# A spectrum's return from DRAM cut into growing blocks, output blocks in halves, and the order around them rewritten

## The chip, the cores and the metric

One core of a Trainium2 chip runs one program. Its five engines work side by side, each through its own list of instructions in order: PE (TensorE, matrix products), ACT (ScalarE), DVE (VectorE), POOL (GpSimd) and SP (SyncE, which issues the transfers). The metric is the time of one execution in microseconds on the device, the median of the runs.

## The reference, cut to what matters

Input q is normalised and modulated, gates a long convolution, and the sum goes through a second normalisation and a gated linear unit. S = 2048 rows, D = 448 channels, F = 1792; all float32.

```python
mod = (_silu(c) @ w_mod).reshape(c.shape[0], 6, 1, -1)
sa, ca, ga, sb, cb, gb = ...
h = _layernorm(x) * (1 + ca) + sa            # LN1, modulation
k_shift = short causal convolution of k (4 taps); kv = k_shift * v
y = irfft(rfft(kv) * rfft(ssm_k))[:S] + kv * ssm_D
x = x + ga * (h * y)
h = _layernorm(x) * (1 + cb) + sb            # LN2, modulation
x = x + gb * ((sigmoid(h @ w_gate) * (h @ w_up)) @ w_down)
```

## The kernel before, in words

The channels are worked in two halves of 224 (h = 0 and 1), the 2048 rows as 16 tiles of 128 rows. The FFT is made of small matrix products. Stage 1 transforms along one axis; `av[h]`, 128 partitions x 32 slots x 224 channels, holds the spectrum of kv, `ak[h]` that of the filter. Between stages the 32 x 32 blocks of (row in a group of 32 partitions, slot) must be transposed. For some channel blocks DVE does that (`turn`, line 181, and the transposing read at line 339); for the first 112 channels of each half a return trip through DRAM does it: slots are written out to `kd0` or `kd1` and read back with row and slot exchanged.

The stretch that matters is `stage2_v` (line 306): 16 late steps p = 8h + n, eight channel blocks for each half. In each step PE makes the block's products `s2v` (line 316), DVE multiplies them with the filter's spectrum (`m`, line 320), PE transforms the product of the step before (`sa`, line 336, in `stage2_back`), which ACT copies into `av` (line 341) or DVE transposes into it (line 339). Then `beside` (line 682) does what else stands in that step, by tables on p: `TURNS`, the sums of the modulation vectors (`mod_parts`, `mod_sum`), the filter's own `s2k` products and ACT's copy of them (`stage2_k`, line 287; copy at line 291), LN1's statistics on ACT (`ln1_stats`, line 449; two tiles at a time, each a sum and a sum of squares), LN1's reciprocal and product on DVE (`ln1_end`, line 459), the gates on POOL and ACT (`gates`, line 466), and from step 12 on one output block of the first half per step (`stage_out`, line 354: 16 products; one call makes y0 for four tiles, written `y0_0` to `y0_3`; y1 is the second half's).

The second half's trip goes so: `eight_out` (line 346) writes eight slots of all 128 partitions to `kd1` in each of the steps 9 to 12, and in step 13 `half_in` (line 349) reads back all 32 slots in four transfers, one for each group of 32 partitions, 1024 pieces of 448 bytes each. These are issued by SP, in order, on one queue. The program uses eight DMA semaphores in turn: an issue waits until the transfer eight issues before it has landed, and everything behind it on SP waits too.

After step 15 come the last transform sa7, the y1 blocks (the first needs the returned spectrum), the vectors of modulation 3 and 5, the second half's gate, LN2's statistics (`ln2_stats`), the normalised rows (`norm_rows`), the turns of four row tiles through PE (`turn_one`, line 951; column group 1 is 64 wide and is turned twice, once for each half of the partitions, with a transpose and a product), and then the products of gate and up (`gu`, line 1004) with weights that are split into a high and a low part (`plain_hi` on ACT, `plain_lo`, line 532, on POOL for three of the first four pieces). From there on PE goes from gate products to down products (`d`, line 925) to the end.

Everything runs in the written order (`tc.manual_schedule()`, line 536): no scheduler moves anything. Buffers in PSUM are named by tags; tag `y`, `sa` and two of `t` go round.

Of the kernel before, what the change touches and what calls it, by code (L numbers as in the profile page):

```python
# [17 lines left out]
P = 128  # L18
C = 224
# [60 lines left out]
def adaln_conv_glu_kernel(ctx: ExitStack, tc: tile.TileContext, q, kT, v, ssm, shift, dskip,  # L80
# [225 lines left out]
    def stage2_v(between, last):  # L306

        for h in range(2):
            for n in range(8):
# [14 lines left out]
                between(h, n)  # L324
        last()
        stage2_back()

    def stage2_back():
# [3 lines left out]
        for b in range(2):  # L332
            for ex in range(2):
                r = slice(64 * ex, 64 * ex + 64)
                y = pt[r, b, :D] if not straight else pt[r, b].rearrange("p (j c) -> p j c", c=32)[:, :, :28]
                PE.matmul(y, wa[:, b, r], m[b][:, ex], start=True, stop=True)  # L336
# [4 lines left out]
        ACT.activation(block(av[h], h, n), cols4(rows(pt), h, n), AF.Copy)  # L341
# [4 lines left out]
    def eight_out(a, scratch, n, c):  # L346
        nc.sync.dma_start(scratch[:, 8 * n:8 * n + 8, c], a[:, 8 * n:8 * n + 8, c])

    def half_in(a, scratch, c, *bs):
        x = scratch.rearrange("(b q) p c -> b p q c", b=4)  # L350
        for b in bs:
            nc.sync.dma_start(a[32 * b:32 * b + 32, :, c], x[b, :, :, c])

    def stage_out(h, i, tag, cs=slice(0, C), pt=None):

        pt = two(tag, f"y{h}_{i}") if pt is None else pt
        for b in range(2):
            for jj in range(2):
                g = 4 * i + 2 * b + jj
                for s in range(2):  # L360
                    PE.matmul(pt[64 * s:64 * s + 64, b, jj * C + cs.start:jj * C + cs.stop], wb[:, 16 * s + g], av[h][:, 16 * s + g, cs], start=True, stop=True)  # L361
        return rows(pt)
# [33 lines left out]

    def mod_parts(m, tag, part=None):

        pr = two(tag, f"mod{m}")
        for h in range(2):  # L400
# [3 lines left out]
        if part is None:  # L404
            part = late["rb"].tile([P, D], F32, tag="part", bufs=1, name=f"part{m}")
        ACT.activation(part, pr[:, 0, :D], AF.Copy)
        mods[m] = pr, part

    def mod_sum(m):

        pr, part = mods.pop(m)
        if m not in (3, 4):
            PE.matmul(pr[:, 1, :D], ones, part, start=True, stop=True)
            if m == 2:
                DVE.tensor_mul(arow, arow, pr[:, 1, :D])
                DVE.tensor_mul(brow, brow, pr[:, 1, :D])
            else:
                ACT.activation({1: arow, 0: brow, 5: gbrow}[m], pr[:, 1, :D], AF.Copy, bias=1.0 if m == 1 else 0.0)
            return
        at, add = (0, 1.0) if m == 4 else (5, 0.0)  # L420
# [27 lines left out]

    def ln1_stats(k):

        for i in range(2 * k, 2 * k + 2):
            t, g = late["x1"][:, i], slice(i, i + 1)
            ACT.activation(gbrow, t, AF.Copy, scale=-1.0 / D, accum_out=nmr[:, g])
            ACT.activation(gbrow, t, AF.Square, bias=nmr[:, g], accum_out=rstd[:, g])
        if k % 2:
            r = rstd[:, 2 * k - 2:2 * k + 2]
            ACT.activation(r, r, AF.Sqrt, bias=eps, scale=1.0 / D)

    def ln1_end(i):
        r, m = rstd[:, 4 * i:4 * i + 4], nmr[:, 4 * i:4 * i + 4]  # L460
        DVE.reciprocal(r, r)
        DVE.tensor_mul(m, m, r)

# [210 lines left out]
    for n in range(2):  # L674
# [4 lines left out]
    TURNS = {0: ((0, 2),), 1: ((0, 3), (1, 0)), 2: ((0, 4), (1, 1)), 3: ((0, 5),), 4: ((0, 6), (1, 2)), 5: ((0, 7),), 6: ((1, 3),),  # L679
             9: ((0, 4), (1, 4)), 10: ((0, 5), (1, 5)), 11: ((1, 6),), 12: ((1, 7),)}  # L680

    def beside(h, n):

        p = 8 * h + n
        if p in (3, 4, 7, 10):
            ln1_end({3: 0, 4: 1, 7: 2, 10: 3}[p])
        for at in TURNS.get(p, ()):
            turn(av[at[0]], at[1])
        for m in {0: (0,), 1: (1,), 3: (2,), 10: (4,)}.get(p, ()):
# [28 lines left out]
        if p in (0, 1, 2, 3, 5, 6, 8, 9):  # L718
            ln1_stats(p if p < 4 else p - 1 if p < 7 else p - 2)
        if p >= 12:  # L720
            y = stage_out(0, p - 12, "y")
            if p < 14:
                gate(0, p - 12, y_copy(0, p - 12, y), POOL)
            elif p == 14:
                y = late["g02"] = y_copy(0, 2, y)
                POOL.tensor_mul(y, y, pairs(gt[0, 2]))
            else:
                late["y03"] = y

    def first_forms():  # L730
        late["g03"] = copy_home(3)
        DVE.tensor_mul(late["g03"], pairs(gt[0, 3]), late["y03"])
# [8 lines left out]
    plain_hi(0, 3)  # L741
    parts = slice(0, 7 * 28), slice(7 * 28, C)
    y10 = [stage_out(1, 0, "t", parts[0])]
    mod_parts(3, "sa")
    mod_parts(5, "y", gbrow)
    y10.append(stage_out(1, 0, "t", parts[1]))
    four = lambda x, c: pairs(x).rearrange("p b (j c) -> p b j c", c=C)[:, :, :, c]
# [3 lines left out]
    for c in parts:  # L751
        xs_ = late["x1"][:, 0:4, C + c.start:C + c.stop]
        DVE.tensor_add(xs_, xs_, gt[1, 0][:, :, c])
    mod_sum(3)
    mod_sum(5)
    gate_wd(0)
    yc = []
    y1 = [None, stage_out(1, 1, "t")]
    y1.append(stage_out(1, 2, "t"))
    ln2_stats(0, 1, 2, 3, act=(0,))  # L760
    load_gu(1, 0, 2)
    ln2_end(0, 1)
    yc.append(y_copy(1, 1, y1[1]))
    rb_.close()
    pg_.close()
# [177 lines left out]

    load_wd(1, wdraw)
    norm_rows(0)
    yc.append(y_copy(1, 2, y1[2]))

# [3 lines left out]
    def turn_one(t, pt):  # L951
        at, w = AT[t]
        for i in range(4):
            PE.transpose(pt[0:w, i * P:(i + 1) * P], xn[:, i, at:at + w], ident)
            if w < P:
                PE.matmul(pt[w:P, i * P:(i + 1) * P], xn[:, i, at:at + w], ident, start=True, stop=True)

    p0 = ps.tile([P, 512], F32, tag="y", name="pt_0")
    p2 = ps.tile([P, 512], F32, tag="t", bufs=2, name="pt_2")
    turn_one(0, p0)  # L960
    turn_one(2, p2)
    p13 = two("t", "pt_13")
    norm_hi(0, p0, xf["B11"][:, 0])
    norm_hi(2, p2, xf["B21"][:, 0])
    plain_lo(0, 3)
    load_gu(1, 2, 4)
    DVE.tensor_mul(pairs(gt[1, 1]), pairs(gt[1, 1]), yc[0])
    norm_full(0, 0, p0)
    turn_one(1, p13[:, 0])
    turn_one(3, p13[:, 1])  # L970
    norm_full(0, 1, p13[:, 0])
    norm_full(0, 3, p13[:, 1])
    norm_full(0, 2, p2)
    DVE.tensor_copy(xf["B11"][:, 1], full[:, 1])
    DVE.tensor_copy(xf["B21"][:, 1], full[:, 3])
    x_lo("B11")
    x_lo("B21")
    gate_add(1, 1, gt[1, 1], DVE)
    split_plain(1, 0, 1)
    ln2_stats(4, 5, 6, 7, act=(4,))  # L980
    split_plain(1, 2, 3)
    ln2_end(4, 1)
    norm_rows(1, (1, 3))

# [12 lines left out]
    def plain_half(p, q, n, f, between=None):  # L997
# [4 lines left out]
        for i, (m, g) in enumerate(ops):  # L1002
            t, s, b, k = order[m]
            PE.matmul(pt[:, g], plain(q, t)[:, s, g, f * P:f * P + P], xf[xs_[b]][:, k], start=m == 0, stop=m == 10, skip_group_check=True)  # L1004
            if i == (10 if p else 7) and between:
                between()
        sg = st[p % 2 * 2][:, f]
        ACT.activation(sg, pt[:, 0], AF.Sigmoid)
        if p == f == 0:
            norm_rows(1, (0, 2))  # L1010
        DVE.tensor_mul(sg, sg, pt[:, 1])
# [21 lines left out]
    act_stats = lambda *k: ln2_stats(*k, act=k)  # L1033
    do = lambda f, *k, **w: lambda: f(*k, **w)
    def last_block():
        y1.append(stage_out(1, 3, "y"))
        yc.append(y_copy(1, 3, y1[3]))

    turns = {(0, 0): last_block, (1, 0): do(turn_full, 1, 0, 1), (1, 1): do(turn_full, 1, 2, 3)}
    ends = {(0, 0): [do(split_wd_hi, 0, 0), do(split_wd_lo, 0, 0)],  # L1040
            (0, 1): [do(gate_wd, 1, DVE), do(gate, 1, 2, yc[1], DVE)],
            (1, 0): [lambda: gate(1, 3, yc[2], DVE), do(split_wd_hi, 1, 1), do(split_wd_lo, 1, 1), do(load_wd, 2, wdraw), do(load_raw, 2)],
# [225 lines left out]
```

## Time and profile before

| | us |
|---|---|
| median of the runs (574.95 to 577.49) | 575.09 |
| the profiled execution | 575.48 |
| its span | 573.7 |
| PE busy in the span | 547.4 (95%) |
| DVE busy | 445.8 (78%) |
| ACT busy | 278.4 (49%) |
| POOL busy | 61.3 (11%) |

The profile shows one execution. The times in it are microseconds from the start of its span; 1.8 us of the execution's own time lie outside the span. A row of the timeline has start, duration, engine, line, operation, output and inputs, count, and in brackets how long the engine stood idle before it and what released it. The chain of waits is followed back from the last instruction. PE's clock was granted in full all along (0.999).

### The profile page before, as it was taken

The page shows a single profiled execution, that of the slowest core. Times are in us where ns is not written, and L with a number is a line of the kernel's source. Part 1 is how long each engine was busy: PE and PEld are TensorE (multiplying, and loading weights), DVE is VectorE, ACT ScalarE, POOL GpSimd, SP SyncE. Part 2 cuts the span into 40 slices and gives each one's busy share as a digit, 9 for nine tenths or more (in the row PEclk, how much of TensorE's full clock was granted, in tenths as well). Part 3 has the DMA queues.
Part 4 walks back from the last instruction along what each step waited for, and adds up shares of the span by engine and source line. Part 5 has one row for each costly group of instructions (what it writes and reads, how often), then busy time and mean ns, then how long its engine had stood idle before and what let it go on. Part 6 is the DMA issues. An engine that isn't in the chain of part 4 may idle for free.

```text
span 573.7 us, 7812 instructions
## 1 busy us (share of the span) xinstructions
PE 547.4 (95%) x3012; PEld 415.0 (72%) x3012; DVE 445.8 (78%) x528; ACT 278.4 (49%) x479; POOL 61.3 (11%) x54
## 2 busy tenths in 40 slices
PE   7997898999999999997999999999999999999996
PEld 6564432334568888875888888888888888888886
DVE  0899799998787887788888888985555556878564
ACT  4989499782367486447536453242121213333120
POOL 2000007989410000000000000000000000000000
PEclk9999999999999999999999999999999999999999
DMA  8999999788710307487848277676555663220103
GB/s 285 290 304 342 259 249 303 155 200 202 157 58 12 140 22 292 169 293 297 304 172 306 114 270 228 206 262 250 147 175 146 183 216 134 74 102 6 59 0 129
DMA packets 46745, 107.74 MB, mean 188 GB/s; under 512 B 19954, under 2 KB 25076, under 8 KB 45684
## 3 DMA queue, kind: packets, MB, share of 16 engines
q1 hardware_dynamic: 40404, 82.46, 48.6%
q10 hardware_dynamic: 6304, 24.78, 10.9%
q8 instruction: 24, 0.39, 0.3%
q14 instruction: 13, 0.11, 0.1%
HBM read 70.92 MB, written 35.78 MB: 186 GB/s over the span
## 4 chain that ended last, share of the span: by engine, by line
PE 70%; DVE 13%; DMA 9%; ACT 5%; issue 2%; SPq 0%; DVEq 0%; ACTq 0%
PE d L925 22%; PE b L894 15%; PE a L894 10%; PE c L894 10%; DMA inb<-in_v_dram 3%; PE s2v L316 3%; DVE av L183 2%; PE gu L1004 2%; DMA av<-kd 2%; PE sa L336 2%; DMA inb<-in_wgu_dram 1%; DVE m L320 1%; DVE acc L246 1%; DMA kT<-in_kT_dram 1%; PE y L361 1%
## 5 line engine op out<-in xcount | busy, mean ns | idle before, releaser
L925 PE MATMUL d<-wd,h 128*128 128x448 f32 x672 | 145.8, 366 | 2.2 <-DVE x L928 1.5
L925 PEld LDWEIGHTS d<-wd,h 128*128 128x128 f32 x672 | 125.7, 188 | 16.6 <-DVE x L928 2.7
L894 PE MATMUL b<-xt,ring 128*128 128x512 f32 x408 | 99.7, 392 | 2.0 <-DVE st L1135 1.7
L894 PEld LDWEIGHTS b<-xt,ring 128*128 128x128 f32 x408 | 76.1, 188 | 17.7 <-issue 2.0
L928 DVE TENSOR_TENSOR x<-x,d 128x896 f32<-128x896 f32 (+1 forms) x57 | 60.7, 1067 | 19.4 <-PE d L925 19.4
L894 PE MATMUL a<-x,ring 128*128 128x512 f32 x264 | 63.8, 389 | 0.0
L894 PEld LDWEIGHTS a<-x,ring 128*128 128x128 f32 x264 | 49.6, 188 | 10.3
L903 ACT ACTIVATE h<-st 128x512 fp32r<-128x512 f32 x56 | 35.2, 628 | 33.0 <-DVE st L912 20.6
L909 ACT ACTIVATE st<-st 128x512 f32<-128x512 f32 x24 | 15.2, 633 | 73.1 <-DVE st L1177 42.2
L906 DVE TENSOR_TENSOR h<-st,h 128x512 fp32r<-128x512 f32 x56 | 38.5, 687 | 14.5 <-ACT h L903 14.4
L1004 PE MATMUL gu<-x,ring 128*128 128x512 f32 x176 | 41.9, 392 | 0.0
L1156 ACT ACTIVATE st<-st 128x512 f32<-128x512 f32 x12 | 7.6, 632 | 68.1 <-DVE st L1155 68.1
L1004 PEld LDWEIGHTS gu<-x,ring 128*128 128x128 f32 x176 | 32.7, 188 | 6.8 <-DVE x L829 0.3
L320 DVE TENSOR_TENSOR m<-s2v,ak 128x896 f32<-128x896 f32 x32 | 33.3, 1087 | 4.2 <-ACT tmp L369 2.2
L183 DVE STREAM_TRANSPOSE av<-av 128x896 f32<-128x896 f32 x18 | 33.3, 1890 | 2.3 <-ACT av L232 2.3
L316 PE MATMUL s2v<-av,w 64*64 64x448 f32 x256 | 32.1, 546 | 2.8 <-DVE m L320 2.1
L894 PE MATMUL c<-x,ring 128*128 128x512 f32 x144 | 34.7, 390 | 0.0
L875 ACT ACTIVATE ring<-sum 128x512 fp32r<-128x512 f32 x28 | 17.3, 626 | 35.4 <-DVE sum L856 18.3
L894 PEld LDWEIGHTS c<-x,ring 128*128 128x128 f32 x144 | 27.0, 188 | 5.2
L894 PE MATMUL c<-xt,ring 128*128 128x512 f32 x120 | 29.1, 389 | 0.0
L336 PE MATMUL sa<-m,wa 128*64 128x448 f32 x128 | 27.5, 551 | 0.0
L912 DVE TENSOR_TENSOR st<-st 128x512 f32<-128x512 f32 x24 | 16.6, 690 | 12.5 <-ACT st L909 12.4
(179 smaller groups left out, 782.5 us busy)
## 6 DMA issues: line engine op xcount, KB each, us to landing
fd<-ring ACTq DMA_DIRECT2D x35, 512.0 KB, 3.7
ring<-fd SPq DMA_DIRECT2D x35, 512.0 KB, 3.7
wdk<-wd ACTq DMA_DIRECT2D x7, 896.0 KB, 3.6
wd<-wdk SPq DMA_DIRECT2D x7, 896.0 KB, 4.7
inb<-in_wgu_dram SPq DMA_DIRECT2D x6, 1024.0 KB, 5.3
kdk<-ak SPq DMA_DIRECT2D x4, 896.0 KB, 7.8
ak<-kdk SPq DMA_DIRECT2D x16, 224.0 KB, 8.0
x<-in_q_dram SPq DMA_DIRECT2D x4, 896.0 KB, 11.8
```

Source lines behind the costliest of these rows:

```text
L183: DVE.transpose(x, x)
L316: PE.matmul(pts[b][c:c + 64, ex, :D], w2[r:r + 64, ex], x[r:r + 64, b], start=True, stop=True)
L320: DVE.tensor_mul(cols4(m[b], h, n), cols4(rows(pts[b]), h, n), k[:, b].unsqueeze(1).to_broadcast([P, 2, D // w, w]))
L336: PE.matmul(y, wa[:, b, r], m[b][:, ex], start=True, stop=True)
L875: ACT.activation(forms[name, i][:, 0], w_src(name), AF.Copy)
L894: PE.matmul(pt, wh(s, t), x[:, k], start=start and m == 0, stop=stop and m == len(ops) - 1, skip_group_check=True)
L903: ACT.activation(hh, h, AF.Copy)
L906: DVE.tensor_sub(hl, h, hh)
L912: DVE.tensor_mul(y[:, 0], y[:, 0], y[:, 1])
L925: PE.matmul(pt[:, i, :D], h[:, (2 * e + i) * P:(2 * e + i + 1) * P], x, start=m == 0, stop=m == len(ops) - 1)
L928: DVE.tensor_add(y, y, rows(pt)[:, a:b])
L1004: PE.matmul(pt[:, g], plain(q, t)[:, s, g, f * P:f * P + P], xf[xs_[b]][:, k], start=m == 0, stop=m == 10, skip_group_check=True)
```

## The change

It has four parts.

*Blocks.* `half_in` of the second half is replaced by `blocks_in`. After each `eight_out` of slots 8n to 8n + 7, one step later, it reads the part of the transposed square that is now complete: for each group of 32 partitions rows 8n to 8n + 7 with slots 0 to 8n + 7, and rows 0 to 8n - 1 with slots 8n to 8n + 7. That makes 4, 8, 8 and 8 transfers in steps 10 to 13.

*Halves.* `stage_out` can make one half of a block (two of its four tiles). y0_0 moves to step 10, y0_1 is made in halves in steps 12 and 13, y0_2 in step 14 and behind sa7, y0_3 around the first y1 block. For that the turns (0, 5) and (1, 4) change places between steps 9 and 10.

*LN1.* The product in `ln1_end` goes to ACT for two of the four groups (steps 4 and 7) as four activations of one column, and from step 4 on a step's statistics stand half before and half behind the s2k copy.

*From the vectors to the gate products.* `plain_lo` of three weight pieces goes from POOL to DVE, behind the first two normalised tiles; `gate_wd(0)` goes from POOL to DVE; the 64-wide column group is first doubled by DVE (`dup`) and turned as a full one; modulation 5 is summed behind eight gate products; `load_wd(1)` is issued behind the loads of the second weight group; the order of what DVE does beside the first gate products is new.

The core of the diff:

```diff
+    def blocks_in(a, scratch, n, c):
+        x = scratch.rearrange("(b q) p c -> b p q c", b=4)
+        i, j = 8 * n, 8 * n + 8
+        for b in range(4):
+            if n:
+                nc.sync.dma_start(a[32 * b:32 * b + i, i:j, c], x[b, 0:i, i:j, c])
+            nc.sync.dma_start(a[32 * b + i:32 * b + j, 0:j, c], x[b, i:j, 0:j, c])
...
-    def ln1_stats(k):
+    def ln1_stats(k, rows_=(0, 1)):
-        for i in range(2 * k, 2 * k + 2):
+        for i in [2 * k + r for r in rows_]:
...
     def ln1_end(i):
...
-        DVE.tensor_mul(m, m, r)
+        if i in (0, 3):
+            DVE.tensor_mul(m, m, r)
+        else:
+            for k in range(4):
+                ACT.activation(m[:, k:k + 1], m[:, k:k + 1], AF.Copy, scale=r[:, k:k + 1])
...
-             9: ((0, 4), (1, 4)), 10: ((0, 5), (1, 5)), 11: ((1, 6),), 12: ((1, 7),)}
+             9: ((0, 4), (0, 5)), 10: ((1, 4), (1, 5)), 11: ((1, 6),), 12: ((1, 7),)}
...
+        if p > 3 and p in STATS:
+            ln1_stats(STATS[p], (0,))
         if 4 <= p < 12:
             stage2_k(1, p - 4, "sa" if p in (9, 10) else "y")
...
+        if 10 <= p < 14:
+            blocks_in(av[1], kd1, p - 10, half)
...
-        if p == 13:
-            half_in(av[1], kd1, half, *range(4))
...
+        for i, b_ in {10: ((0, (0, 1)),), 12: ((1, (0,)),), 13: ((1, (1,)),), 14: ((2, (0,)),)}.get(p, ()):
...
-        for t in (2, 0, 1):
-            plain_hi(0, t)
-        for t in (2, 0, 1):
-            plain_lo(0, t, POOL)
+        plain_hi(0, 2)
...
+    stage_out(0, 2, "y", pt=late["y0"], b_=(1,))
+    half_gate(2, 1)
...
     y10 = [stage_out(1, 0, "t", parts[0])]
+    late["y0"] = two("y", "y0_3")
+    stage_out(0, 3, "y", pt=late["y0"], b_=(0,))
+    y10.append(stage_out(1, 0, "t", parts[1]))
     mod_parts(3, "sa")
...
-    gate_wd(0)
...
-    load_wd(1, wdraw)
     norm_rows(0)
+    dup(DVE)
...
-            PE.transpose(pt[0:w, i * P:(i + 1) * P], xn[:, i, at:at + w], ident)
-            if w < P:
-                PE.matmul(pt[w:P, i * P:(i + 1) * P], xn[:, i, at:at + w], ident, start=True, stop=True)
+            PE.transpose(pt[:, i * P:(i + 1) * P], xn[:, i, at:at + P] if w == P else xd[:, i], ident)
...
     norm_hi(2, p2, xf["B21"][:, 0])
...
+    plain_lo(0, 2)
+    plain_lo(0, 0)
+    plain_lo(0, 1)
+    load_gu(1, 0, 2)
     plain_lo(0, 3)
     load_gu(1, 2, 4)
...
+    load_wd(1, wdraw)
...
+            if i == 7 and p == f == 0:
+                last_vector()
```

SP's list from the third `eight_out` on (`kd1<-av1`) in the kernel before; the third number group is partitions x slots x channels of the piece written:

```order
L347 DMA kd1_691<-av1_399 128x8x112
L500 DMA tmp_1056<-in_wd_dram 128x896
L347 DMA kd1_691<-av1_399 128x8x112
L352 DMA av1_399<-kd1_691 32x32x112 x4
L392 DMA wm30_1281<-in_wmod_dram 112x896
```

and in the kernel after, from the second to the last transfer of return 2 (n = 2) and the first of return 3:

```order
L356 DMA av1_399<-kd1_691 8x24x112
L355 DMA av1_399<-kd1_691 16x8x112
L356 DMA av1_399<-kd1_691 8x24x112
L355 DMA av1_399<-kd1_691 24x8x112
L356 DMA av1_399<-kd1_691 8x32x112
```

Four transfers of 32 partitions behind the fourth `eight_out` have become sixteen of 8, 16 or 24; the eight of return 2 and the eight of return 3 both stand behind the fourth `eight_out`, those of return 1 behind the third.

PE's list from the last y0 block to the sum of modulation 5 before (y0 and y1 are output blocks, sa1_7 the last transform, mod3 and mod5 vectors):

```order
L361 MATMUL y0_3_1271<-av0_398,wb_92 64x224 x8
L336 MATMUL sa1_7_1292<-m1_7_0_1261,wa_669 64x16x28 x2
L336 MATMUL sa1_7_1292<-m1_7_1_1262,wa_669 64x16x28 x2
L361 MATMUL y1_0_1299<-av1_399,wb_92 64x196 x8
L403 MATMUL mod3_1308<-wm30_1281,scb_89 32x224 x4
L403 MATMUL mod3_1308<-wm31_1283,scb_89 32x224 x4
L403 MATMUL mod5_1319<-wm50_1103,scb_89 32x224 x4
L403 MATMUL mod5_1319<-wm51_1105,scb_89 32x224 x4
L361 MATMUL y1_0_1329<-av1_399,wb_92 64x28 x8
```

and the same place after:

```order
L337 MATMUL sa1_7_1297<-m1_7_0_1285,wa_669 64x16x28 x2
L337 MATMUL sa1_7_1297<-m1_7_1_1286,wa_669 64x16x28 x2
L370 MATMUL y0_2_1270<-av0_398,wb_92 64x224 x4
L370 MATMUL y1_0_1318<-av1_399,wb_92 64x196 x8
L370 MATMUL y0_3_1327<-av0_398,wb_92 64x224 x4
L370 MATMUL y1_0_1332<-av1_399,wb_92 64x28 x8
L412 MATMUL mod3_1341<-wm30_1300,scb_89 32x224 x4
L412 MATMUL mod3_1341<-wm31_1302,scb_89 32x224 x4
L370 MATMUL y0_3_1327<-av0_398,wb_92 64x224 x4
```

Half of y0_2 now stands between the last transform and the first y1 block, and the two halves of y0_3 stand behind that block's first part.

ACT's list around step 8 before (s2k copies into `ak1`, statistics into `nmr` and `rstd`, the copy of the transform `sa1_0`):

```order
L291 ACTIVATE ak1_149<-s2k1_3_968 128x8x112
L474 ACTIVATE inb_75<-x1_626,nmr_97,rstd_96 128x224 x4
L291 ACTIVATE ak1_149<-s2k1_4_1007 128x32x28
L453 ACTIVATE gbrow_93,nmr_97<-x1_626 128x448
L454 ACTIVATE gbrow_93,rstd_96<-x1_626,nmr_97 128x448
L453 ACTIVATE gbrow_93,nmr_97<-x1_626 128x448
L454 ACTIVATE gbrow_93,rstd_96<-x1_626,nmr_97 128x448
L341 ACTIVATE av1_399<-sa1_0_1031 128x8x112
```

and after:

```order
L480 ACTIVATE nmr_97<-nmr_97,rstd_96 128x1 x4
L291 ACTIVATE ak1_149<-s2k1_3_974 128x8x112
L492 ACTIVATE inb_75<-x1_626,nmr_97,rstd_96 128x224 x4
L467 ACTIVATE gbrow_93,nmr_97<-x1_626 128x448
L468 ACTIVATE gbrow_93,rstd_96<-x1_626,nmr_97 128x448
L291 ACTIVATE ak1_149<-s2k1_4_1015 128x32x28
L467 ACTIVATE gbrow_93,nmr_97<-x1_626 128x448
L468 ACTIVATE gbrow_93,rstd_96<-x1_626,nmr_97 128x448
L342 ACTIVATE av1_399<-sa1_0_1037 128x8x112
```

Four one-column activations have come in, and one tile's statistics stand ahead of the s2k copy instead of behind it.

More of the change, by code (lines that the diff above doesn't have):

```diff
@@ L324, in stage2_v, with stage2_back @@
                 between(h, n)
-        last()
-        stage2_back()
-    def stage2_back():
+        stage2_back(last)
+    def stage2_back(between=None):
         h, n, m = products.pop(0)
@@ L332, in stage2_back @@
         for b in range(2):
+            if b and between:
+                between()
             for ex in range(2):
@@ L395, in adaln_conv_glu_kernel, with mod_parts @@
     mods = {}
-    def mod_parts(m, tag, part=None):
-        pr = two(tag, f"mod{m}")
+    def mod_parts(m, tag, part=None, copy=True):
+        pr = two(tag, f"mod{m}") if type(tag) is str else tag
         for h in range(2):
@@ L405, in mod_parts, with mod_copy, mod_sum @@
             part = late["rb"].tile([P, D], F32, tag="part", bufs=1, name=f"part{m}")
+        mods[m] = pr, part
+        if copy:
+            mod_copy(m)
+    def mod_copy(m):
+        pr, part = mods[m]
         ACT.activation(part, pr[:, 0, :D], AF.Copy)
-        mods[m] = pr, part
-    def mod_sum(m):
+    def mod_sum(m, copy=True):
         pr, part = mods.pop(m)
@@ L454, in ln1_stats @@
             ACT.activation(gbrow, t, AF.Square, bias=nmr[:, g], accum_out=rstd[:, g])
-        if k % 2:
+        if k % 2 and 1 in rows_:
             r = rstd[:, 2 * k - 2:2 * k + 2]
@@ new lines, in beside, with half_gate @@
+        if p == 15:
+            half_gate(2, 0)
+        for i, b_ in {10: ((0, (0, 1)),), 12: ((1, (0,)),), 13: ((1, (1,)),), 14: ((2, (0,)),)}.get(p, ()):
+            if 0 in b_:
+                late["y0"] = two("y", f"y0_{i}")
+            y = stage_out(0, i, "y", pt=late["y0"], b_=b_)
+            if 1 not in b_:
+                continue
+            gate(0, i, y_copy(0, i, y), POOL)
+    def half_gate(i, b):
+        y = copy_home(i)[:, b]
+        ACT.activation(y, rows(late["y0"])[:, b], AF.Copy)
+        POOL.tensor_mul(y, y, pairs(gt[0, i])[:, b])
@@ L742, in adaln_conv_glu_kernel @@
+    late["g02"], late["g03"] = copy_home(2), copy_home(3)
     parts = slice(0, 7 * 28), slice(7 * 28, C)
     y10 = [stage_out(1, 0, "t", parts[0])]
+    late["y0"] = two("y", "y0_3")
+    stage_out(0, 3, "y", pt=late["y0"], b_=(0,))
+    y10.append(stage_out(1, 0, "t", parts[1]))
     mod_parts(3, "sa")
-    mod_parts(5, "y", gbrow)
-    y10.append(stage_out(1, 0, "t", parts[1]))
+    y = stage_out(0, 3, "y", pt=late["y0"], b_=(1,))
+    ACT.activation(late["g03"], y, AF.Copy)
+    POOL.tensor_mul(late["g03"], late["g03"], pairs(gt[0, 3]))
```

93 lines of the change are left out of this document (44 added, 49 removed).

## The prediction

> **What bounds the kernel now.** I read the busy time by windows first, to see from where on nothing but TensorE (PE) counts; columns are PE, weight loads, DVE, ACT, POOL, clock, DMA share, GB/s.
>
> ```profile
> 168.00:206.00 38.00, 38.00 (x182) 31.52 (x178) 32.56 (x46) 23.31 (x45) 0.00 (x0) 1.00 0.25 87
> 206.00:241.00 35.00, 34.78 (x159) 29.37 (x158) 29.08 (x38) 21.32 (x41) 0.00 (x0) 1.00 0.45 173
> 241.00:265.00 24.00, 19.98 (x87) 15.49 (x86) 19.92 (x30) 12.71 (x21) 0.00 (x0) 1.00 0.83 313
> 265.00:573.70 308.70, 302.94 (x1408) 261.21 (x1406) 225.31 (x270) 102.95 (x160) 0.00 (x0) 1.00 0.49 167
> ```
>
> From 168 us PE is busy without a gap to 206 and nearly so to the end; the one hole (4.0 us in 241:265) comes from work that PE's own progress sets off. Nothing of the diff lies behind 206. So the change is worth the time by which PE reaches the gate products earlier or later, if DVE and ACT then keep up. Next the chain of waits ahead of them.
>
> ```profile
> 137.01 1.54 PE y L361 x16
> 138.55 0.80 SPq L352
> ...
> 139.40 11.05 DMA av<-kd
> ...
> 150.69 1.55 PE y L361 x16
> ...
> 159.83 0.51 DVE xn L792
> ...
> 162.23 0.36 PE pt L956 x2
> ...
> 164.37 0.59 PE pt L954 x4
> 164.96 1.16 PE gu L1004 x5
> ```
>
> The end hangs on the return of the second half's spectrum (`half_in`): 11.05 us of DMA, behind which the first y1 product starts at 150.69. I call that start S. From S to the first gate product (gu) it is 14.3 us. PE's own rows say how long it stood there.
>
> ```profile
> 148.02 1.67 PE L336 MATMUL sa<-m,wa 128*64 128x448 f32 x8
> 150.69 1.55 PE L361 MATMUL y<-av,wb 128*64 128x196 f32 x16 [1.00 <-DMA av<-kd]
> ```
>
> Only 1.00 us: sa7 ended at 149.69. Without the wait S could move by 1.0 us, and further only if PE's work ahead of it shrinks too.
>
> **The change part by part.** *LN1's product to ScalarE.*
>
> ```profile
> 92.94 2.09 POOL L483 TENSOR_TENSOR G<-G,brow 128x896 f32<-128x896 f32 x1
> 93.26 1.79 DVE L462 TENSOR_TENSOR nmr<-nmr,rstd 128x4 f32<-128x4 f32 x1
> 99.57 2.72 PE L316 MATMUL s2v<-av,w 64*64 64x448 f32 x16 [2.09 <-DVE m L320]
> 110.24 0.16 DVE L462 TENSOR_TENSOR nmr<-nmr,rstd 128x4 f32<-128x4 f32 x1
> 117.68 0.98 PE L285 MATMUL s2k<-ak,w 64*64 64x448 f32 x8 [0.64 <-ACT av L341]
> 123.68 0.98 PE L285 MATMUL s2k<-ak,w 64*64 64x448 f32 x8 [0.77 <-ACT av L341]
> 158.72 0.48 ACT L444 ACTIVATE rstd<-mv,cols 128x1 f32<-128x1 f32 x2
> ```
>
> At step 4 the product of four numbers took DVE 1.79 us, until the POOL operation beside it ended; at step 7 (110.24), with POOL idle, 0.16. PE waits for DVE soon after (99.57). So up to 1.79 us is gained there; on ACT eight activations at 0.24 us (half of 0.48) come in, 1.9 us, and in steps 8 to 10 PE waits for ACT (0.64 and 0.77). The statistics, split around the s2k copy, leave the `av` copy that PE waits for behind one tile of statistics and not two. I take −1.2 us; bounds −1.8 (all of DVE's gain) and +0.5 (1.9 less the 1.4 of those two waits, nothing gained). The two turns that change places between steps 9 and 10 let y0 start at step 10 and are covered by the same waits.
>
> *Blocks in halves.* Before, four y0 blocks of 1.54 us stand between the s2v products; now two and a half, and the third's other half behind sa7, so one block (1.54) moves behind S. PE is then ready for y1 at 149.69 − 1.2 − 1.54 = 146.95.
>
> *From S to the gate products.*
>
> ```profile
> 179.22 1.08 PE L812 MATMUL pt<-ident,xn 128*128 128x128 f32 x8
> 147.99 3.75 POOL L534 TENSOR_TENSOR ring<-tmp,ring 128x512 fp32r<-128x512 f32 x3 [1.50 <-ACT ring L530]
> 170.40 1.28 DVE L534 TENSOR_TENSOR ring<-tmp,ring 128x512 fp32r<-128x512 f32 x2
> 165.81 0.43 DVE L974 CAST x<-full 128x512 fp32r<-128x512 f32 x1 [0.96 <-ACT full L817]
> 183.53 1.08 DVE L504 TENSOR_TENSOR wdraw<-wdraw,gbrow 128x896 f32<-128x896 f32 x1
> 179.16 0.43 DVE L801 COPY xn<-xn 128x512 f32<-128x512 f32 x1 [0.61 <-ACT xn L794]
> 168.56 0.35 SPq L500 DMA_DIRECT2D wdraw<-in_wd_dram  x1
> 168.96 0.42 SPq L496 DMA_DIRECT2D tmp<-in_wgu_dram  x1
> 173.59 1.15 ACT L530 ACTIVATE ring<-tmp 128x512 fp32r<-128x512 f32 x2 [1.55 <-DMA tmp<-in_wgu_dram]
> ```
>
> PE: the y0 block comes in (+1.54); the narrow turns (162.23 to 164.37, 2.14 us) become four whole ones of 0.135 (eight in 1.08), −1.60. DVE: `dup` moves ahead of the turns (0.43, beside the first two turns), three `plain_lo` come from POOL, which had them hidden (3 x 0.64 = 1.92), and `gate_wd(0)` (1.08); two casts go (0.86), so does the 0.96 that DVE waited for ACT there, and ACT's wait of 1.55 for a weight load, which `load_wd(1)` held up on SP's queue until the last y1 block was read; that load now goes first, and `load_wd(1)` waits with nothing urgent behind it. Sum: −0.06 on PE, 3.43 − 3.37 = +0.06 on the DVE and ACT side. The vector sum of mod 5 only changes places with eight gate products. I take 0; bounds −1.0 (a gain of one removed wait) and +1.9 (the `plain_lo` uncovered, since the second gate product needs the first of them).
>
> *The return in blocks.* Bytes are the same, 1.84 MB; the transfers are 28 and not 4, and in 24 of them 8 or 16 rows are written at a time, in the last four 24. Rates by windows, then SP's rows:
>
> ```profile
> 75.00:76.00 1.00, 1.00 (x6) 0.30 (x6) 1.00 (x2) 0.94 (x5) 0.00 (x0) 1.00 0.97 343
> 81.00:82.00 1.00, 1.00 (x18) 0.41 (x12) 1.00 (x2) 1.00 (x1) 0.00 (x0) 1.00 1.12 220
> 97.00:102.00 5.00, 2.88 (x24) 0.68 (x16) 5.00 (x4) 4.44 (x11) 4.84 (x4) 1.00 1.15 294
> 111.00:116.00 5.00, 5.00 (x38) 1.57 (x34) 4.74 (x5) 4.28 (x11) 4.84 (x6) 1.00 1.20 205
> 140.00:148.00 8.00, 8.00 (x68) 3.93 (x66) 6.65 (x6) 1.63 (x3) 5.86 (x4) 1.00 1.20 179
> ```
> ```profile
> 128.81 0.39 SPq L347 DMA_DIRECT2D kd<-av  x1
> 133.18 0.38 SPq L347 DMA_DIRECT2D kd<-av  x1
> 137.36 4.00 SPq L352 DMA_DIRECT2D av<-kd  x4
> ```
>
> Writing 32 partitions goes at 205 and 179 GB/s with 448-byte pieces (`half_in` of both halves) and at 220 with 896-byte ones (81:82, `turn_in`). Yet 448-byte pieces leave all 128 partitions at 294 (97:102, `half_out`) and loads into all of them run at 343. So the piece is not what limits a return: the number of partitions written does. Nor do transfers into other partitions run beside: four `half_in` are in flight together and move 205. That makes 6.4 GB/s a partition: 51 for 8 partitions, 103 for 16, 154 for 24. The other end is that 205 holds for any shape.
>
> The Trainium skill bears on that. SBUF — State Buffer, section "Door 1: The DMA port swizzle", says that bandwidth follows the DMA ports that a transfer's partitions reach, 27 GB/s a port, eight ports for 32 neighbouring partitions (189 GB/s measured there; 205 here agrees) and by its map two for eight. Its 54 GB/s would shorten the sum below by 1.5 us, an estimate.
>
> The sum from rows. The third `eight_out`, at 128.81 before, goes out at 128.81 − 1.2 + 1.54 = 129.15; its bytes are out some 2.5 us later, 131.7 (as from 133.18 to 137.36 the fourth took 4.2 to be complete). Then follow on the one queue: return 1 (8 rows only, 344 KB at 51) 6.7; the weight load and the fourth `eight_out` (0.46 MB each at 294) 3.1; return 2 (344 KB at 51, 229 KB at 103) 8.9; return 3 (459 KB at 51, 344 KB at 154) 11.2. That ends at 161.6, complete 0.8 later: 162.4. If the wider pieces of returns 2 and 3 run beside the narrow ones, 4.4 less: 158.0. I take the middle, S = 160.2, 9.5 us later than 150.69. At 205 for all, returns 2 and 3 take 2.8 and 3.9 us; the fourth `eight_out`, issued near 134.3 behind the program's wait for an older transfer, is complete at 138.5, and return 3 lands near 145: PE's 146.95 then sets S.
>
> Sum: 575.48 (the profiled execution, span 573.7 and 1.8 around it) + 9.5 + 0 = 585.0. The median of the runs, 575.09, lies 0.4 lower, so 584.6; all times below are on that scale.
>
> **The rivals.** *The blocks land in time* (the other side: faster). Any shape moves at 205 GB/s, S = 146.95, −3.7: 571.4. For it: the returns' bytes are the same, and over half of them can go before the last `eight_out`. Against it: 205 and 220 where pieces differ twofold, 294 and 343 where partitions differ. It decides at about 100 GB/s for the 8-row pieces: above that PE no longer waits longer than now.
>
> *Half the rate.* The 8-row pieces move at half of 205: return 1 3.4, return 2 3.4 + 1.1, return 3 4.6 + 2.3, all at 149.5, complete 150.3; S −0.4: 574.7. If each of the 16 last issues takes 1.0 us as in the row of four (4.00), they end at 150.3 and land near 152.3, 576.7. For it: the row of issues; against: that row's four hold 1024 pieces each, the new ones at most 256.
>
> The skill's page DMA: Bandwidth & Descriptors, section "Why a DMA increments its semaphore by 16 and not by 1", gives a reason for just this rate: a transfer is split over the largest number of engines up to 16 that divides its outer dimension, so 8 rows go over eight. No row here shows a transfer of 8 rows, so neither page is tested yet.
>
> *DVE becomes the bound behind S.* The moved `plain_lo` and `gate_wd` are not covered: +1.9 on top of a case, 573.3 with blocks in time. For it: DVE's 32.56 of 38.00 in 168:206.
>
> **How the numbers follow.** A difference under 0.5% (2.9 us) can't be told from none. Forecast (partitions limit) 0.53, its own range 580 to 588 (S from 156 to 163.5). Half the rate or issue cost 0.20. Blocks in time 0.27, of which 0.04 with DVE's cost. 572.2 is the border to faster: blocks in time 0.23. Within 0.5%: 0.20 and that 0.04, 0.24. Slower: 0.53. As blocks in time hold more than two in ten, the range reaches to them: 571.0 to 588.0.
>
> **What the profile after would show.** Right: 8-row transfers at 50 to 60 GB/s in 140:158, PE standing at the first y1 product some 10 us for a DMA, gu first at 174. Step 4 without the 1.79 us on DVE. Wrong: GB/s near 200 during the returns and the first y1 product at 147 with no wait; then the partition rate is what failed. A gu start more than 14.5 us behind S would say that DVE's new work is not covered.

## The result, and the profile after

The changed kernel takes 582.38 us (581.68 to 582.89, four runs) where the kernel before takes 575.02 on the same chip: ratio 1.0118, interval 1.0088 to 1.0148, so it is slower. The profiled execution's span is 580.6 us, 6.9 more than before.

PE's timeline of the changed kernel shows where the 6.9 us are (rows as before):

```profile
142.41 3.28 PE L337 MATMUL sa<-m,wa 128*64 128x448 f32 x16
145.52 0.93 PE L370 MATMUL y<-av,wb 128*64 128x224 f32 x8
157.15 5.36 PE L370 MATMUL y<-av,wb 128*64 128x196 f32 x40 [10.70 <-issue]
...
171.78 2.16 PE L1028 MATMUL gu<-x,ring 128*128 128x512 f32 x8
```

PE is ready for the first y1 product at 146.45, 3.2 us sooner than before, and then stands 10.70 us. S is 157.15 and was 150.69: +6.46. The gate products come 14.63 us behind S and came 14.27 behind it: +0.36. Behind them nothing changes (408.8 us to the end, 408.7 before). The chain of waits names what PE stood for:

```profile
128.84 0.39 SPq L348
...
134.32 0.39 SPq L348
...
135.37 6.29 DMA av<-kd
141.68 7.43 DMA av<-kd
```

The third and the fourth `eight_out` go out at 128.84 and 134.32, and behind them the chain is transfers of the return up to 149; its last 6.7 us are put down to the next vector's load (`wm`), issued behind the return, and PE's row names no releaser (`issue`). The view of `av` has PE's weight loads for y1 wait 11.1 us for `av`, and pieces under 512 bytes (the return's have 448) move until 155.6. That the wait is for the return is shown below: a_whole and a_16 differ from this kernel only in how the return is cut, and there the row names it. The rates by windows (length, PE, weight loads, DVE, ACT, POOL, granted clock, DMA share, GB/s):

```profile
136.00:137.00 1.00, 1.00 (x12) 0.49 (x12) 1.00 (x2) 0.21 (x1) 1.00 (x1) 1.00 0.92 311
...
138.00:139.00 1.00, 1.00 (x12) 0.34 (x6) 0.65 (x2) 0.00 (x0) 1.00 (x1) 1.00 1.19 283
139.00:140.00 1.00, 1.00 (x8) 0.39 (x6) 1.00 (x2) 0.00 (x0) 1.00 (x2) 1.00 1.02 129
...
142.00:143.00 1.00, 1.00 (x12) 0.34 (x6) 0.68 (x2) 0.00 (x0) 0.92 (x2) 1.00 0.64 60
...
144.00:145.00 1.00, 1.00 (x8) 0.31 (x6) 1.00 (x2) 0.26 (x1) 1.00 (x2) 1.00 0.66 73
...
146.00:147.00 1.00, 0.44 (x6) 0.04 (x2) 1.00 (x2) 0.51 (x2) 0.00 (x0) 1.00 0.64 90
...
148.00:149.00 1.00, 0.00 (x0) 0.00 (x0) 0.00 (x0) 0.59 (x2) 0.25 (x1) 0.91 0.63 107
149.00:150.00 1.00, 0.00 (x0) 0.00 (x0) 0.00 (x0) 0.00 (x0) 0.00 (x0) 0.50 0.84 65
...
161.00:162.00 1.00, 1.00 (x17) 1.00 (x14) 0.30 (x1) 0.00 (x0) 0.00 (x0) 0.50 0.00 0
162.00:163.00 1.00, 1.00 (x20) 0.80 (x22) 0.45 (x2) 0.00 (x0) 0.00 (x0) 0.77 0.00 0
163.00:164.00 1.00, 1.00 (x20) 0.53 (x10) 0.90 (x3) 0.53 (x1) 0.00 (x0) 1.00 0.00 0
```

The fourth `eight_out` and the weight load still move at 311 GB/s; the returns behind them at 60 to 107 until 150 (then the vector's load runs beside them), where `half_in` had 179. And there is a column that the prediction had not looked at: the granted clock, as a share of full speed, falls to 0.50 at 148.8 (148:149 reads 0.91), 2.4 us after PE's last product, and is full again only at 162.5, 5.3 us after PE has begun to work again.

### The profile page after: what moved, and what is told of

Read it like the earlier page. It is cut to its first block, busy times and chain, and to the rows that moved or that the text cites. A ratio compares the mean times of both kernels' runs of the same rounds, so it can differ in the third digit from the quotient of the medians.

```text
span 580.6 us, 7837 instructions
## 1 busy us (share of the span) xinstructions
PE 547.1 (94%) x3004; PEld 416.3 (72%) x3004; DVE 445.0 (77%) x528; ACT 281.5 (48%) x491; POOL 57.6 (10%) x52
## 4 chain that ended last, share of the span: by engine, by line
PE 72%; DMA 10%; DVE 8%; ACT 7%; issue 3%; SPq 1%; DVEq 0%; ACTq 0%
PE d L955 22%; PE b L924 15%; PE c L924 9%; PE a L924 9%; PE gu L1028 4%; DMA av<-kd 3%; PE s2v L316 3%; PE y L370 2%; DMA kdk<-ak 2%; PE sa L337 1%; PE s2k L285 1%; PE s1k L206 1%; DMA inb<-in_wgu_dram 1%; DVE av L183 1%; DMA wm<-in_wmod_dram 1%
## 5 line engine op out<-in xcount | busy, mean ns | idle before, releaser
L316 PE MATMUL s2v<-av,w 64*64 64x448 f32 x256 | 31.8, 546 | 0.9 <-DVE av L183 0.5
L370 PE MATMUL y<-av,wb 128*64 128x224 f32 (+2 forms) x144 | 16.8, 381 | 10.7 <-issue 10.7
```

The source lines that it names most:

```text
L316: PE.matmul(pts[b][c:c + 64, ex, :D], w2[r:r + 64, ex], x[r:r + 64, b], start=True, stop=True)
```

## The experiments

Two theories had to be told from others: that the blocks' low rate sets S, and that the half clock behind the wait costs time of its own. S and the distance from S to the gate products (gu) are read from each profiled execution; ratios are to the kernel before on the same chip. It took 576.1 to 576.4 beside the experiments and 575.02 beside the changed kernel, so the ratios are to be compared and not the times.

| kernel | S | S to gu | us | ratio, interval |
|---|---|---|---|---|
| before | 150.69 | 14.27 | 575.02 | 1 |
| after | 157.15 | 14.63 | 582.38 | 1.0118 (1.0088 to 1.0148) |
| a_whole | 149.16 | 13.75 | 573.58 | 0.9951 (0.9933 to 0.9970) |
| a_16 | 152.87 | 14.84 | 578.42 | 1.0042 (1.0026 to 1.0057) |
| b_blocks | 160.95 | 16.07 | 587.11 | 1.0193 (1.0158 to 1.0229) |
| a_warm | 163.99 | 12.00 | 587.44 | 1.0190 (1.0165 to 1.0215) |
| a_warm12 | 156.61 | 12.19 | 580.44 | 1.0073 (1.0044 to 1.0102) |
| b_ln1 | 149.32 | 14.34 | 574.22 | 0.9960 (0.9939 to 0.9980) |
| a_two | 146.75 | 12.39 | 569.59 | 0.9877 (0.9854 to 0.9900) |
| b_two | 150.24 | 13.72 | 574.94 | 0.9987 (0.9971 to 1.0003) |
| a_two_pool | 146.37 | 12.56 | 570.33 | 0.9905 (0.9885 to 0.9924) |
| a_two_narrow | 146.15 | 13.63 | 570.82 | 0.9912 (0.9893 to 0.9930) |

Where one row of the timeline holds the half of y0_2 and the first y1 block together (a_two and its kin), S is that row's start plus 0.85, which is what the half takes in the others until the next row starts.

### What limits a return: m_shapes

```diff
-    (the whole computation)
...
+    for b in range(4):
+        put(S_, b, 24, 32)
+    mark(4)
+    for k in range(4):
+        for b in range(4):
+            put(S_, b, 8 * k, 8 * k + 8)
+    mark(5)
```

`put` is `half_in`'s transfer for some rows of a group, `mark` a small DVE read of all that has landed. There are fifteen such sets.

> Leaves the whole computation out: only transfers from DRAM into av, all issued by SP and each set read by DVE before the next goes out, so a set's time is the stretch from its first issue to that DVE read. Pieces of 448 bytes. Three theories of what sets the rate, with 205 GB/s for four transfers of 32 rows (1.84 MB, 9.0 us plus some 2 us of start) common to them. Partitions written (6.4 GB/s each and no two transfers side by side): four of 24 rows 8.9 us, four of 16 rows 9.0, four of 8 rows 9.0, all 128 rows in sixteen transfers of 8 rows 36. DMA engines (a transfer goes over the largest number up to 16 that divides its rows): 9.0 for 24 rows (12 engines), 4.5 for 16 rows, 4.5 for 8 rows, 18 for the sixteen. Issue and start only, 205 GB/s for any shape: 6.7, 4.5, 2.2 and 9.0. If exchanged rows in DRAM are the limit, the sets without the exchange are faster at the same rows; if one queue is, two queues halve the time.

DVE's timeline of m_shapes; the bracket is how long DVE waited for a set, from the end of the read before:

```profile
44.72 0.18 DVE L103 COPY see<-av 128x32 f32<-128x32 f32 x1 [11.09 <-DMA av<-kd]
55.07 0.19 DVE L103 COPY see<-av 128x32 f32<-128x32 f32 x1 [10.16 <-DMA av<-kd]
65.35 0.19 DVE L103 COPY see<-av 128x32 f32<-128x32 f32 x1 [10.10 <-DMA av<-kd]
97.31 0.19 DVE L103 COPY see<-av 128x32 f32<-128x32 f32 x1 [31.77 <-DMA av<-kd]
124.94 0.19 DVE L103 COPY see<-av 128x32 f32<-128x32 f32 x1 [27.45 <-DMA av<-kd]
136.30 0.19 DVE L103 COPY see<-av 128x32 f32<-128x32 f32 x1 [11.17 <-DMA av<-kd]
...
185.18 0.19 DVE L103 COPY see<-av 128x32 f32<-128x32 f32 x1 [18.03 <-DMA av<-kd]
196.02 0.19 DVE L103 COPY see<-av 128x32 f32<-128x32 f32 x1 [10.65 <-DMA av<-kd]
```

Four transfers of 24 rows take 11.1 us, of 16 rows 10.2, of 8 rows 10.1: the time does not ask how many rows there are. All 128 rows in sixteen transfers of 8 take 31.8, and 27.5 when one group of 32 comes behind the other; four of 32 rows on two queues (groups 0 and 2 on SP, 1 and 3 on ACT) 11.2. Pieces of 896 bytes take 18.0 for twice the bytes, and rows not exchanged 10.7, so neither the length of a piece nor the exchange counts. The first theory's 8.9, 9.0 and 9.0 fit, with a start of some 1 to 2 us added (one transfer of 32 rows alone takes 4.24 us, four 11.16); its 36 for the sixteen is too high, since they move at 58 GB/s and not at 51. The engine theory's 4.5 for 16 and for 8 rows and the issue theory's 2.2 are refuted. A transfer of 8 neighbouring rows costs 31.8 / 16 = 2.0 us for 32 slots, 62 ns a slot.

### Partitions or ports: m_ports

```diff
+    def step(eng, b, r0, k):
+        eng.dma_start(av[32 * b + r0:32 * b + 32:k, :, c], x[b, r0:32:k, :, c])
...
+    for b in (0, 2, 1, 3):
+        put((S_, S_, A_, A_)[b], b, 0, 32)
+    mark(2)
```

> Leaves the whole computation out: transfers from DRAM into av alone, pieces of 448 bytes, each set read by DVE before the next goes out. The sets with contiguous rows showed a time that goes with the bytes for one partition and not with the rows (four of 32 rows 11.4 us, four of 8 rows 10.1). Two theories say why. One partition's own limit (7 GB/s each, one transfer at a time): 8 rows with stride 4 take as long as 8 rows side by side, 10 us for four; 16 rows with stride 2 the same; groups 0 and 1 on SP beside groups 2 and 3 on ACT gain nothing, 11 us and 31. Ports shared by four neighbouring partitions, the same for groups 0 and 1 and others for groups 2 and 3: 8 rows with stride 4 reach eight ports, not two, 4 to 6 us for four of them, and 16 transfers of them 10 to 16 where sixteen of 8 neighbours took 31.8; groups 0 and 1 on SP beside 2 and 3 on ACT run at once, 6 to 7 us for four of 32 rows and 16 to 18 for sixteen of 8.

DVE's timeline of m_ports: four of 32 rows on two queues (0 and 1, 2 and 3), on one queue; sixteen of 8 neighbours on two queues; four of 8 neighbours, of 8 rows with stride 4, of 16 with stride 2; sixteen of 8 with stride 4.

```profile
42.55 0.19 DVE L103 COPY see<-av 128x32 f32<-128x32 f32 x1 [9.11 <-DMA av<-kd]
53.90 0.19 DVE L103 COPY see<-av 128x32 f32<-128x32 f32 x1 [11.16 <-DMA av<-kd]
77.12 0.19 DVE L103 COPY see<-av 128x32 f32<-128x32 f32 x1 [23.04 <-DMA av<-kd]
87.21 0.19 DVE L103 COPY see<-av 128x32 f32<-128x32 f32 x1 [9.91 <-DMA av<-kd]
93.17 0.19 DVE L103 COPY see<-av 128x32 f32<-128x32 f32 x1 [5.77 <-DMA av<-kd]
100.77 0.19 DVE L103 COPY see<-av 128x32 f32<-128x32 f32 x1 [7.42 <-DMA av<-kd]
115.72 0.19 DVE L103 COPY see<-av 128x32 f32<-128x32 f32 x1 [14.76 <-DMA av<-kd]
```

The same 8 rows' worth of bytes takes 9.91 us into neighbours and 5.77 into every fourth partition; sixteen such take 14.8 and not 31.8. So it is not the number of partitions that counts, as the prediction had it, but that neighbours share a way in. The stride changes the order in DRAM too, but that isn't it: in the set of m_shapes that is not exchanged the eight rows lie far apart in DRAM, and it takes 10.7. Two queues gain 2.0 of 11.2 and 8.7 of 31.8 when they serve groups 0 and 1 beside 2 and 3, less than the half that the port theory gave; why not the half stays open. The Trainium skill, SBUF — State Buffer, section "Door 1: The DMA port swizzle", has the map that fits: four neighbours share a port, partitions 0 to 31 have the ports of 32 to 63, and 64 to 127 have the others.

### The blocks in the kernel: a_whole, a_16, b_blocks

a_whole:

```diff
-        if 10 <= p < 14:
-            blocks_in(av[1], kd1, p - 10, half)
+        if p == 13:
+            half_in(av[1], kd1, half, *range(4))
```

> The changed kernel with the return whole, four transfers of 32 rows in step 13, as before the change. Theory (the blocks' low rate sets S, and PE's clock at half speed after its long wait costs some 2.5 us behind S): the return lands as before, S at 150 to 151 and not 157.15; PE is ready at 146.5 and stands about 4 us, so that part of the clock's loss stays; gate products 13 to 14.5 us behind S; 574 to 577. Rival (the blocks cost little and the late S comes from the third vector's load, issued behind them, or from the order of the output blocks): S stays near 156, over 580.

PE's timeline of a_whole:

```profile
145.76 0.93 PE L370 MATMUL y<-av,wb 128*64 128x224 f32 x8
149.16 4.20 PE L370 MATMUL y<-av,wb 128*64 128x196 f32 x40 [2.47 <-DMA av<-kd]
...
162.91 2.15 PE L1028 MATMUL gu<-x,ring 128*128 128x512 f32 x8 [0.41 <-ACT full L847]
```

Measured 573.58, just under the range; S falls by 8.0 us, and the row names the return as what PE waits for. Without the blocks the change is a small gain. In this execution even the wait of 2.47 us halves the clock:

```profile
148.00:149.00 1.00, 0.00 (x0) 0.00 (x0) 0.08 (x1) 0.83 (x2) 0.49 (x1) 0.88 1.06 270
149.00:150.00 1.00, 0.84 (x6) 0.75 (x8) 0.00 (x0) 0.00 (x0) 0.00 (x0) 0.50 0.34 93
...
152.00:153.00 1.00, 1.00 (x20) 0.78 (x18) 0.85 (x1) 0.00 (x0) 0.00 (x0) 0.92 0.00 0
```

It doesn't always: in two of the twelve executions of a_whole the mean granted clock is 1.000, and these took 571.94 and 572.60.

a_16 keeps two returns, of 16 rows, behind the second and the fourth `eight_out`:

```diff
-        if 10 <= p < 14:
-            blocks_in(av[1], kd1, p - 10, half)
+        if p == 11 or p == 13:
+            blocks_in(av[1], kd1, p // 13, half)
...
-        i, j = 8 * n, 8 * n + 8
+        i, j = 16 * n, 16 * n + 16
```

> The changed kernel with two returns instead of four: rows 0 to 15 with slots 0 to 15 behind the second eight_out, the rest behind the fourth, in blocks of 16 rows. Port theory: 16 neighbouring rows reach four ports, a transfer takes as long for its slots as one of 8 or 32 rows (four of 16 rows and 32 slots 10.2 us); behind the fourth eight_out stand 4 x (16 + 32) slots at 64 ns, 12.3 us from about 138, so S near 150.5, PE stands 4 us, half clock behind: 574 to 577. Engine theory (16 rows on 16 engines run at the full 205 GB/s): lands near 146, 569.5 to 571.

PE's timeline of a_16:

```profile
152.87 5.28 PE L370 MATMUL y<-av,wb 128*64 128x196 f32 x40 [6.02 <-DMA av<-kd]
...
167.71 2.15 PE L1028 MATMUL gu<-x,ring 128*128 128x512 f32 x8 [0.41 <-ACT full L847]
```

578.42 us, over the range, and S 152.87: on the port theory's side, but 2.4 us later than its sum, since the second return is issued only at 139.62 (the fourth `eight_out`, out at 133.30, lands late behind the first return) and takes the 12.3 us and a start from there. At the engine theory's rate it would have landed near 147.

b_blocks puts the blocks alone into the kernel before (`blocks_in` as in the change, `half_in` of step 13 taken out).

> The kernel before with the return in blocks alone. Theory: the return lands near 156 to 157 as in the changed kernel, since eight_out of slots 16 to 23 goes out at the same time (128.8); PE stands 6 to 7 us from 149.7 on, the granted clock falls to half, and the gate products come 14.3 us plus up to 2.5 behind S, near 172: 581 to 584. Rival (the other parts of the change are the slower ones): within 2 us of 575.

587.11, over the range, with executions from 584.41 to 589.75. PE's timeline of b_blocks shows two waits ahead of the return:

```profile
77.13 1.73 PE L336 MATMUL sa<-m,wa 128*64 128x448 f32 x8 [2.00 <-DMA wa<-in_wat_dram]
...
100.58 4.06 PE L316 MATMUL s2v<-av,w 64*64 64x448 f32 x16 [2.07 <-DVE m L320]
...
160.95 3.08 PE L369 MATMUL y<-av,wb 128*64 128x196 f32 x16 [8.91 <-DMA wm<-in_wmod_dram]
```

A weight came 2.00 us late in step 2, ahead of any block, and behind the wait of 2.07 us in step 6 the same products took 4.06 us, not 2.72, at a granted clock of 0.50. So its third `eight_out` goes out at 131.16 and not 128.81, 2.35 us late. From that `eight_out` to S it is 29.8 us, and 28.3 in the changed kernel. So the sign and most of the size stand, but of the 11 us that b_blocks loses in its times (576.08 to 587.11) some 2 may not be the blocks'.

### The half clock: a_warm and a_warm12

```diff
+    p10 = two("t", "y1_0a")
+    for i in range(12):
+        PE.matmul(p10[:, 1, :D], ones, x1[:, 15], start=True, stop=True)
-    y10 = [stage_out(1, 0, "t", parts[0])]
+    y10 = [stage_out(1, 0, "t", parts[0], pt=p10)]
```

a_warm has 23 of them:

> The changed kernel with 23 products that nobody reads (128 x 448, into the first y1 block's own PSUM bank) while PE waits for the return. Theory: S stays at 157.1 to 157.5, the granted clock stays full, and the stretch from S to the gate products falls from 14.6 to about 12.2 us: 579.5 to 580.5. Rival (behind S the vector work on DVE and ACT sets the pace and the clock costs nothing): 582 to 583.

That was mis-sized: each product is two matmuls of 0.38 us, so they lasted 17.6 us and set S themselves, 163.99. The distance to the gate products fell to 12.00 all the same. With 12:

> The changed kernel with 12 products that nobody reads (128 x 448, two matmuls of 0.38 us each, 9.2 us in all) while PE waits for the return; with 23 they went on to 164 and set S themselves. Theory: S at 157.1 to 157.5, full clock, 12.0 us from S to the gate products as with 23, gate products near 169.3: 579.5 to 580.5. Rival (DVE and ACT set the pace there and the clock costs nothing): 582 to 583.

PE's timeline of a_warm12:

```profile
146.58 9.29 PE L773 MATMUL y_0a<-x,ones 128*128 128x448 f32 x24
156.61 1.58 PE L370 MATMUL y_0a<-av,wb 128*64 128x196 f32 x15 [0.74 <-DMA wm<-in_wmod_dram]
...
168.80 2.16 PE L1031 MATMUL gu<-x,ring 128*128 128x512 f32 x8
```

S stays where the return lands, the clock is full, and the gate products come 12.19 us behind S, not 14.63: the half clock costs 2.4 us. 580.44 against 582.38 in another measurement: the ratios 1.0073 and 1.0118 have intervals that overlap, so the trace carries this more than the times do.

### A return that does not wait: a_two and b_two

The edit as b_two makes it in the kernel before; a_two puts the same lines in the place of `blocks_in`:

```diff
         if p == 13:
-            half_in(av[1], kd1, half, *range(4))
+            for eng, bs in ((nc.sync, (0, 1)), (ACT, (2, 3))):
+                half_in(av[1], kd1, half, *bs, eng=eng)
```

> The changed kernel with the return whole in step 13, groups 0 and 1 issued by SP and groups 2 and 3 by ACT. Port theory: the return takes 6 to 8 us and not 12.8, lands by 145 behind an issue at 136.4 to 137.4, PE does not wait for it, S at 146.5, the clock stays full, gate products 12 to 12.5 us behind S, near 159: 569 to 571. Partition theory, or one limit for all engines: it lands near 149 as with one queue, 573 to 574.5.

PE's timeline of a_two:

```profile
142.80 3.28 PE L337 MATMUL sa<-m,wa 128*64 128x448 f32 x16
145.90 3.70 PE L370 MATMUL y<-av,wb 128*64 128x224 f32 x48
...
159.14 2.15 PE L1029 MATMUL gu<-x,ring 128*128 128x512 f32 x8 [0.41 <-ACT full L848]
```

No wait any more: 569.59 us, ratio 0.9877, faster than both kernels. By m_ports two queues save 2.0 us of the return; a_whole's wait was 2.47, and the last thing that PE's weight loads for this block now wait for is DVE's part of `av` (0.41 us), not the return.

> The kernel before with its whole return on two queues, groups 0 and 1 issued by SP and 2 and 3 by ACT. Theory: the return lands near 147 and PE no longer waits for it, but it is ready only at 149.7, so S gains 1.0 us of the 150.7 and no more: ratio 0.998 to 0.999. Rival (the return alone bounds this stretch): ratio 0.995 or less, like the changed kernel with two queues, whose 0.9877 would then owe little to the other edits.

In the kernel before the same edit gives 574.94, ratio 0.9987, which can't be told from none: PE came 1.0 us before the return there and could gain no more; S came 0.45 earlier, at 150.24, because sa7 itself ended later in this profile. So a_two's gain is not the return's alone; it needs PE to be ready early, which is what the rest of the change does.

### The smaller terms: b_ln1, a_two_pool, a_two_narrow

b_ln1 is the kernel before with `ln1_end`, `ln1_stats` and the `STATS` calls of the change, and nothing else.

> The kernel before with LN1's product on ACT for two groups and the statistics split around the s2k copy, nothing else. Theory: the 2.09 us that PE stands for DVE at step 6 goes, the steps from there on and the return with them come 1.2 to 1.8 us earlier: ratio 0.997 to 0.998. Rival (ACT's eight new activations give it back in steps 8 to 10): ratio 1.000 to 1.001.

PE's timeline of b_ln1:

```profile
146.62 1.67 PE L336 MATMUL sa<-m,wa 128*64 128x448 f32 x8
149.32 1.55 PE L361 MATMUL y<-av,wb 128*64 128x196 f32 x16 [1.02 <-DMA av<-kd]
```

sa7 ends at 148.29, 1.40 sooner than before, and S moves by 1.37 with the whole trip. The ratio 0.9960 says 2.3 us, beyond the expected 0.997, but its interval reaches from 1.2 to 3.5 us and holds the 1.4 of the trace. The wait in step 6 that goes with this edit halved the clock in b_blocks and not in the profile before; whether that adds to the gain is not shown.

a_two_pool moves the three `plain_lo` back behind the `plain_hi`, on POOL; a_two_narrow turns the 64-wide group as before and drops the first `dup`.

> The changed kernel with the return on two queues, and the three weight pieces' low parts back on POOL. Theory (the 1.92 us that DVE took over are covered by PE's gate products): same as with them on DVE, 569.3 to 570.0. Rival (DVE's list is what the first down product waits for, 0.48 us in the trace): 0.5 to 1.5 us faster.

> The changed kernel with the return on two queues, and the 64-wide column group turned narrow again, twice, without the doubling on DVE. Theory: PE's 1.60 us come back on its path, less what the doubling's 0.43 us frees: 1.2 to 1.6 us slower, 570.8 to 571.2. Rival (DVE and ACT set that stretch): same.

570.33, above the range, and 570.82, in it. The eighth group of down products starts 82.31 us behind S with POOL (228.68 − 146.37) and 82.17 with DVE (228.92 − 146.75): up to there the three pieces are covered. By the medians POOL is 0.7 us slower than a_two, on another chip and with intervals that overlap; in the trace the difference comes at 259, where PE waits 1.56 us for DVE and not 1.05, and why it does is open. With narrow turns the eighth group starts 83.41 behind S (229.56 − 146.15), 1.24 later than in a_two, as expected.

## Why the prediction was right

582.38 lies in the likeliest case's own range. The 2.2 us between it and 584.6 are S (157.15, not 160.2: −3.05), the way to the gate products (+0.36), behind them (+0.1), and the 0.4 by which the scale of the medians had been set lower.

*LN1, −1.2.* Right: −1.40 in b_ln1.

*PE ready at 146.95.* Right: 146.45. The two `eight_out` were put at 129.15 and 134.3 and went out at 128.84 and 134.32.

*The return, S at 160.2.* The mechanism was right in its size and not in its name. Eight rows were put at 51 GB/s and move 459 KB in four transfers in 10.1 us, or 58 GB/s without a change of set (1.84 MB in 31.8 us). But 8 rows with stride 4 take 5.8, so "the number of partitions written does" is wrong: neighbours share a way in. For rows side by side the two rules give nearly the same times, which is why the sum held. S came 0.9 ahead even of the sum's early end, 158.0. What the sum missed is at its start: return 1, the weight load and the fourth `eight_out` were put one behind the other until 141.5, yet the wide transfers move at 311 GB/s beside return 1's end. Returns 2 and 3 have 4 x (8 + 24) + 4 x (8 + 32) = 288 slots, 17.9 us at 62 ns; back from 157.15 that is a start at 139.3. The rate falls there, from 283 GB/s in 138:139 to 129 in 139:140. The 0.8 us that the sum put behind the last byte stood on no row; here the last pieces under 512 bytes move at about 155.6, 1.6 before S. The estimate from the ports of the Trainium skill's page SBUF — State Buffer, 54 GB/s, put S 1.5 us sooner than the sum, and the runs are on its side.

*The test "50 to 60 GB/s in 140:158".* It was badly put: the window holds the wide pieces and the next vector's load, and reads 60 to 107 by the microsecond from 140 to 150 and 69 to 185 behind. The 10 us that PE would stand were 10.70.

*From S to the gate products, 0.* The sum came out, +0.36, by luck: two terms that were both missed cancel. At full clock the new order is ahead by 14.27 − 12.19 = 2.1 us at the gate products. Of these 0.9 only change places (the sum of modulation 5, now behind eight of them). At the eighth group of down products a_two is 0.65 us ahead of the kernel before (82.17 against 82.82), and at the end of the span 1.7 (421.35 us behind S against 423.01), beyond the bound of −1.0. Against that the clock takes 2.4 back, and it was not in the sum at all. The rule "more than 14.5 us behind S would say that DVE's new work is not covered" would have misled: 14.63 was measured, a_two_pool shows that work covered up to the down products, and a_warm12 shows the clock as the cause.

*The rivals.* Blocks in time: refuted, 205 GB/s at any shape would have S at 147. Half the rate over eight engines: refuted by m_shapes, where 16 rows take as long as 8 (10.2 and 10.1 us), and by a_16's S of 152.87. The issue cost of 1.0 us: the rows of SP show 0.3 to 1.1 each, in most cases about 0.3, with waits for older transfers between them. DVE as the bound behind S: not seen, a_two_pool is no faster.

## What to carry to other kernels

Before a transfer is cut to start earlier, price each piece by the bytes that it brings to one partition: for 8 to 32 neighbouring partitions the time went with these and not with the number of partitions, so cutting by rows made more transfers that each took as long for their slots as a whole one, and the last one landed later. A wait of PE of some 2 us can cost twice, once for itself and once at the half clock behind it, and doesn't always; read the granted clock by the microsecond around each such wait. And free what comes last first: in a_whole PE was ready 3.0 us sooner than before (146.69 for 149.69), but S came only 1.5 sooner (149.16); the rest came when the return landed sooner too, in a_two (146.75).

## What the runs showed of the hardware

The clock column of the profiles shows waits of PE in which, or just behind which, it fell to half:

| run | PE stands from | clock falls at | stands till then, us | clock full again at | at half, us |
|---|---|---|---|---|---|
| a_two_pool | 45.83 | 47.5 | 1.6 | 50.9 | 3.4 |
| a_whole | 146.69 | 148.76 | 2.1 | 152.16 | 3.4 |
| after | 146.45 | 148.8 | 2.4 | 162.5 | 13.6 |
| b_blocks, y1 | 152.04 | 155.5 | 3.5 | 165.8 | 10.2 |
| a_16 | 146.84 | 151.1 | 4.2 | 157.9 | 6.8 |

In b_blocks it also fell at 100.9, 2.4 us after the products ahead of step 6 had ended, for 3.4 us. The stretches at half are one, two, three and four times 3.4 us. The length of the wait alone doesn't decide: waits of 2.09 us (step 6 of the kernel before), 2.00 (step 2 of b_blocks) and 1.57 (the kernel before, up to 46.99, the same place as in a_two_pool) left the clock full. The Trainium skill, TensorE: Matmul & The Clock Gate, Part 1, gives the watched window 3.4 us and lets it run freely; the multiples agree, and so does the chance in it, while its "after ≥1 idle window (~3.4µs)" is longer than the 1.6 to 2.4 us that were enough in four of these six cases.

Two queues moved the same transfers faster only where they served partitions 0 to 63 beside 64 to 127 (9.1 and 8.7 us against 11.2; with groups 0 and 2 on one queue and 1 and 3 on the other, 11.2).
